# Rounded weights finished by a transfer instead of a sum: a recurrent layer and an MLP on one core

## The chip, the core and the metric

The kernel runs on one NeuronCore of a Trainium2 chip. A core has a matrix engine (PE; its weight loads are shown on a row of their own, PEld), a vector engine (DVE), an engine for activation functions (ACT), a general-purpose engine (POOL) and a sequencer for transfers (SP). Transfers between HBM and the on-chip memory (SBUF), or within it, run on 16 shared DMA engines; SP, ACT and POOL issue them, each through a queue of its own. Matrix products land in PSUM, from where DVE and ACT read them. Every engine takes its instructions in order, and waits where an instruction needs a semaphore that has not come.

The metric is the time of one execution on the device in microseconds. Before the change it is 679.25 us, the median of three runs (678.58, 679.25 and 681.2).

## The reference

Attention first: for each of 4 sequences and 8 heads, over 768 steps, a complex state of 48 x 48 decays and takes in a product of key and value, and the query reads its real part. Then an MLP with an ELU, in float32 or better:

```python
mag = np.sqrt(a_re * a_re + a_im * a_im)
scale = np.minimum(mag, 0.999) / (mag + 1e-06)
...
for t in range(S):
    ar, ai = (a_re_n[:, :, t, :, None], a_im_n[:, :, t, :, None])
    new_re = ar * S_re - ai * S_im
    new_im = ar * S_im + ai * S_re
    kv = np.einsum('bhd,bhe->bhde', k[:, :, t], v[:, :, t])
    S_re, S_im = (new_re + kv, new_im)
    y[:, :, t] = np.einsum('bhd,bhde->bhe', q[:, :, t], S_re)
...
h = x @ w_in                                           # x: 3072 x 384, w_in: 384 x 2048
g = np.where(h > 0.0, h, alpha * (np.exp(np.minimum(h, 0.0)) - 1.0))
return (g @ w_out).astype(np.float32)                  # w_out: 2048 x 384
```

The two weight matrices arrive as float64. They are rounded to float32 on the chip, from the two 32-bit words of each number.

## The kernel before

The 3072 tokens are worked through in groups `u` of 256 (two sequences of 128 steps each, so 12 groups). For each group the kernel loads q, k, v and the complex decay, forms gates from logarithms, angles and sums along time (`squares` to `gated`), transposes, scores and state products on PE (`transposed`, `scores`, `states`, `values`), moves some rows of the result into place by small transfers (`seam`, issued by POOL, ACT and SP), and passes the result `x` through the first layer (`inner`, L1202), the ELU (`elu`, L1215) and the second layer (`project`, L1225). From group 2 or 3 on the layers use sums of blocks of the weights, prepared once on DVE from the rounded ones (`summed_in`, `combined`), and fewer products.

The weights are fetched and rounded in 16 blocks of 128 partitions x 768 numbers: eight of w_in ("in" 0 to 7) and eight of w_out ("out" 0 to 7). `fetch` (L641) has SP load the raw words of a block into one of two buffers `w64` (the first blocks of "in" borrow others); a fetch waits until the block two earlier has been read. `rounded` (L647) then rounds it on DVE: `_rounded` (L36) masks and shifts the high word into a float32 `wf`, truncated (L40, L43), takes its exponent (L46) and multiplies by it the low word, scaled, which gives the rest that was cut off, `wp` (L50); a fifth step, L655, adds the two and writes the sum into w_in or w_out. That sum rounds. `wf` and `wp` come from one pool of two buffers, `wt`. `rounded` is a generator: each `convert()` in the order advances it by one step, so a block takes five of them.

The order of the work is written out by hand for the first groups: the list `first` (from L1576) names each step, and each engine receives its instructions in the order in which the list's steps issue them. A `convert` puts one instruction on DVE; an `inner` puts six matrix products on PE (one piece of 256 hidden features, `f` and `f + 1`) into one of three PSUM banks `mlp`, which the `elu` of an earlier piece must have released; an `elu` puts two instructions on ACT and one (L1221) on DVE. After the first groups the steps are ordered by due times (`put`), which the change doesn't touch. A piece `inner(u, f)` needs block f // 2 of w_in, and `project(u, n, f0, f1)` needs the blocks of w_out up to (f1 - 1) // 2. `seam(1)` issues three transfers on POOL and three on ACT.

Of the kernel before, what the change touches and what calls it, by code (L numbers as in the profile page):

```python
# [16 lines left out]
C = 128  # L17
# [14 lines left out]
WF = 2  # L32
# [3 lines left out]
def _rounded(nc, w, f, p):  # L36


    lo, hi = w[:, :, 0], w[:, :, 1]
# [466 lines left out]
def kernel(  # L506
# [140 lines left out]
    def rounded(kind, m):  # L647

        w, dst = raw.pop((kind, m))
        f = sb.tile([C, WF * DM], U32, tag="wt", bufs=2, name="wf")  # L650
        p = sb.tile([C, WF * DM], U32, tag="wt", bufs=2, name="wp")
        yield from _rounded(nc, w, f, p)
        n = dst.shape[-1]
        f, p = (x.bitcast(FP32).rearrange("p (b n) -> p b n", n=n) for x in (f, p))
        nc.vector.tensor_tensor(out=dst, in0=p, in1=f, op=ALU.add)  # L655
        done.append((kind, m))
        yield True
# [912 lines left out]
    def gates_of(u, *at):  # L1570
# [8 lines left out]
        (joined, 0, 0), (squared, "ai", 1), (joined, 0, 1), (logarithms, 0, 0),  # L1579
        (logarithms, 0, 1), (fetch, "in", 1), (fetch, "in", 2), (ratios, 0, 0), (lengths, 0, 0),  # L1580
        (warm, 2), (warm, 1), (lengths, 0, 1), (sums, 1), *2 * [(convert,)],
        (table, "exp_and_others"), (ratios, 0, 1), (powers, 0, 0), (powers, 0, 1), (warm, 2),
        (sums, 0), (warm, 1), (angles, 0, 0), (angles, 0, 1), (summed, 0), (summed, 1),
        (decayed, 0, 0), (turned, 0, 0), (decayed, 0, 1), (turned, 0, 1), (waves, 0, 0),
        (waves, 0, 1), (begun, 1), (warm, 1), (scaled, 0, "q", 0), (ends, 0), (scaled, 0, "k", 0),
        (scaled, 0, "k", 1), (scaled, 0, "q", 1), (warm, 1), (gated, 0, 0), (warm, 1), (noted, 0),
        (table, "natural_log"), (warm, 2), (gated, 0, 1), (warm, 2), *3 * [(convert,)],
        (transposed, 0, "k", 0), (transposed, 0, "q", 1), (carry_on, 0), (transposed, 0, "q", 0),
        *4 * [(convert,)], (scores, 0, 0), (transposed, 0, "k", 1), (scores, 0, 1), (load_a, 1),
        (squares, 1), (joined, 1), (fetch, "in", 3), (logarithms, 1), (states, 0, 0),  # L1590
        (values, 0, 0), (powers, 1), (convert,), (states, 0, 1), (lengths, 1), (load_qk, 1),
        (convert,), (ratios, 1), (values, 0, 1), (seam, 0), (warm, 2), (warm, 2), (decays, 1),
# [156 lines left out]
```

## Time and profile before

| | us |
|---|---|
| median of three runs | 679.25 |
| the profiled execution | 677.98 |
| its span | 676.2 |
| busy: PE, PEld | 642.4, 581.7 |
| busy: DVE, ACT, POOL | 502.3, 419.1, 157.8 |
| L655, the sum, 16 times | 0.95 each, 25.8 to 127.5 us after the span's start |
| L40 and L46, 16 times each | 0.56 each |
| L43 and L50, 16 times each | 0.96 each |

The span is what the engines' records cover; the profiled execution's time is 1.8 us longer. "Busy" counts the time in which an engine has at least one instruction under way. The records are given by line of the kernel, engine, operation and tiles (output first, then inputs). Where an engine was idle before an instruction, a bracket behind it names how long and who released it; "issue" stands for a wait that the profile puts to nobody. In the page's slices each digit is the busy share in tenths of one fortieth of the span. All rounding ends at 128.5 us.

### The profile page before, as it was taken

Reading aid. Unit: us, or ns where it says so; the run is one execution under the profiler, and the core shown is the slowest. Engines: PE = TensorE matmul, PEld = TensorE weight load, DVE = VectorE, ACT = ScalarE, POOL = GpSimd, SP = SyncE. Lnnn points to the kernel's source line nnn. Section 1 sums busy time; section 2 is a strip of 40 time slices with the busy share of each in tenths; the row PEclk is TensorE's granted clock in tenths of the full one; section 3 lists DMA queues with packets and bytes.
Section 4 is the critical chain, followed back from the end, with each engine's and each line's share of the span. In section 5 each row is a group of like instructions: output and inputs, shape, how many; then the busy total and the mean of one; then the engine's idle time right before and its main releaser. Section 6 shows DMA issues by size and latency. Waiting matters only on the chain.

```text
span 676.2 us, 17220 instructions
## 1 busy us (share of the span) xinstructions
PE 642.4 (95%) x7236; PEld 581.7 (86%) x7236; DVE 502.3 (74%) x800; ACT 419.1 (62%) x684; POOL 157.8 (23%) x200
## 2 busy tenths in 40 slices
PE   8899899999997999999999999999999999999995
PEld 6777785577896998998998998998998998999994
DVE  5889999957759678778778778778678777664481
ACT  6875455865854577677677677667677667571350
POOL 2000000122123313503503503504503503402000
PEclk9799999999998999999999999999999999999998
DMA  9995755531900452352441722441642351210000
GB/s 168 175 159 99 144 173 164 82 72 20 153 3 14 93 91 67 77 116 57 102 88 40 147 58 72 104 87 43 116 86 68 75 116 31 66 33 13 18 7 24
DMA packets 151443, 56.12 MB, mean 83 GB/s; under 512 B 129684, under 2 KB 143164, under 8 KB 151356
## 3 DMA queue, kind: packets, MB, share of 16 engines
q1 hardware_dynamic: 147616, 53.58, 39.1%
q0 software_dynamic: 3520, 1.20, 1.8%
q8 instruction: 59, 0.97, 0.6%
q14 instruction: 28, 0.23, 0.1%
q10 hardware_dynamic: 220, 0.14, 0.1%
HBM read 48.91 MB, written 4.80 MB: 79 GB/s over the span
## 4 chain that ended last, share of the span: by engine, by line
PE 53%; DVE 11%; ACT 9%; issue 4%; DMA 2%; SPq 0%; DVEq 0%; ACTq 0%
PE mlp L1319 18%; PE mlp L1450 9%; PE y L1450 6%; PE w L1023 4%; PE mlp L1210 3%; PE w L1064 3%; PE y L1109 3%; DVE g L1466 2%; PE w L837 2%; PE y L1136 2%; DVE g L1475 2%; PE mlp L1235 2%; ACT L735 2%; ACT n L746 1%; DVE g L1297 1%
## 5 line engine op out<-in xcount | busy, mean ns | idle before, releaser
L1319 PE MATMUL mlp<-w_out,g 128*128 128x192 f32 x640 | 113.3, 331 | 1.8 <-DVE ee L1332 1.8
L1319 PEld LDWEIGHTS mlp<-w_out,g 128*128 128x128 f32 x640 | 105.9, 192 | 5.5 <-DVE ee L1332 2.4
L1081 POOL TENSOR_TENSOR S<-S,T 128x384 f32<-128x384 f32 x36 | 33.6, 932 | 178.3 <-DVE S L1079 178.3
L1210 PE MATMUL mlp<-x,w_in 128*128 128x256 f32 x288 | 65.1, 381 | 2.7 <-DVE g L1221 2.4
L1210 PEld LDWEIGHTS mlp<-x,w_in 128*128 128x128 f32 x288 | 53.8, 190 | 11.3 <-DVE g L1221 2.8
L1297 DVE TENSOR_TENSOR g<-g 128x512 f32<-128x512 f32 x80 | 57.7, 731 | 5.0 <-PE mlp L1319 3.8
L1466 DVE TENSOR_TENSOR g<-g,mlp 128x512 f32<-128x512 f32 x45 | 30.7, 683 | 38.2 <-PE mlp L1450 23.9
L1450 PE MATMUL mlp<-x,w_in 128*128 128x128 f32 x432 | 57.2, 275 | 0.0
L1319 PE MATMUL mlp<-w,g 128*128 128x192 f32 x320 | 54.7, 329 | 0.0
L1475 DVE SCALAR_TENSOR_TENSOR g<-ee,g 128x512 f32<-128x512 f32 x63 | 44.1, 700 | 12.2 <-ACT ee L1472 11.9
L1450 PEld LDWEIGHTS mlp<-x,w_in 128*128 128x128 f32 x432 | 52.6, 192 | 0.0
L1319 PEld LDWEIGHTS mlp<-w,g 128*128 128x128 f32 x320 | 51.8, 190 | 0.7
L1471 ACT ACTIVATE ee<-g 128x512 f32<-128x512 f32 x63 | 39.5, 627 | 19.5 <-DVE g L1466 19.3
L1463 ACT COPY g<-mlp 128x512 f32<-128x512 f32 x36 | 21.2, 588 | 43.4 <-PE mlp L1450 43.2
L1472 ACT ACTIVATE ee<-ee 128x512 f32<-128x512 f32 x72 | 45.4, 631 | 2.3
L1190 POOL DMA_DIRECT2D x<-y x62 | 30.1, 493 | 59.4 <-ACT y L1126 37.5
L973 ACT ACTIVATE cs<-n 128x768 f32<-128x768 f32 (+1 forms) x14 | 10.5, 750 | 43.1 <-DVE n L845 43.1
L1024 ACT COPY qt<-w 128x512 f32<-128x512 f32 x48 | 25.8, 589 | 16.0 <-PE w L1023 15.9
L904 ACT ACTIVATE n<-w 64x384 f32<-64x384 f32 (+1 forms) x60 | 28.1, 486 | 8.9 <-PE w L889 8.3
L1450 PE MATMUL y<-x,w_in 128*128 128x128 f32 x216 | 29.3, 278 | 4.0 <-ACT g L1463 4.0
L1450 PEld LDWEIGHTS y<-x,w_in 128*128 128x128 f32 x216 | 26.2, 192 | 4.9 <-ACT g L1463 4.8
L1219 ACT ACTIVATE ee<-mlp 128x512 f32<-128x512 f32 x24 | 14.3, 595 | 25.6 <-PE mlp L1210 16.8
(218 smaller groups left out, 1436.8 us busy)
## 6 DMA issues: line engine op xcount, KB each, us to landing
w<-in_moe_w_out_dram SPq DMA_DIRECT2D x8, 768.0 KB, 4.4
g<-in_moe_w_in_dram SPq DMA_DIRECT2D x24, 256.0 KB, 3.0
g<-in_moe_w_out_dram SPq DMA_DIRECT2D x24, 256.0 KB, 2.9
w<-in_moe_w_in_dram SPq DMA_DIRECT2D x16, 288.0 KB, 5.7
vn<-in_v_dram SPq DMA_DIRECT2D x24, 192.0 KB, 3.9
out_dram<-o SPq DMA_DIRECT2D x48, 96.0 KB, 2.2
ar<-in_a_re_dram SPq DMA_DIRECT2D x22, 192.0 KB, 3.6
ai<-in_a_im_dram SPq DMA_DIRECT2D x22, 192.0 KB, 4.3
```

The source lines that it names most:

```text
L904: nc.scalar.activation(out=flat(x[key][to, n : n + 1]), in_=t[of], func=AF.Exp, scale=sign)
L1023: nc.tensor.transpose(t[:, h], of, ident)
L1081: eng.tensor_tensor(out=new_s, in0=new_s, in1=wide, op=ALU.mult)
L1190: eng.dma_start(out=x["x"][ds(j * HP + D, G), i], in_=x["y"][ds(j * HP + i * G, G)])
L1210: nc.tensor.matmul(t[:, e], lhsT=w_in[:, i, ts(f + e, C)], rhs=x["x"][:, i], start=(i == 0), stop=(i == NI - 1),)
L1297: nc.vector.tensor_tensor(out=S_of(u, k, h), in0=a, in1=b, op=op)
L1319: nc.tensor.matmul(to, lhsT=a[:, m], rhs=b[:, m], start=(first and h == 0 and m == 0), stop=False, skip_group_check=True,)
L1450: nc.tensor.matmul(x["c" + c][:, ts(m, C)], lhsT=a[:, m], rhs=x["mix"][p], start=(p == BANKS[c][0] and m == 0), stop=False, skip_group_che ...
L1466: nc.vector.tensor_tensor(out=part(u, to), in0=part(u, a), in1=part(u, b), op=op)
L1471: nc.scalar.activation(out=e, in_=part(u, of), func=AF.Relu, scale=-1.0)
L1472: nc.scalar.activation(out=e, in_=e, func=AF.Exp, scale=-1.0)
L1475: nc.vector.scalar_tensor_tensor(out=part(u, to), in0=nat[u]["e", to], scalar=-1.0, in1=part(u, of), op0=ALU.add, op1=ALU.max,)
```

## The change

For "in" 2 to 7 and all of "out", fourteen blocks, the fifth step is no longer a sum on DVE. The truncated part is written straight into its place in w_in or w_out (`dst`, read and written there as integers), the rest into `wp`, and POOL issues a transfer from `wp` to `dst` that adds to what stands there. Such a block takes four `convert`s: the fourth puts L50 on DVE and the transfer on POOL's queue. `wf` is no longer allocated for it, so that the two buffers `wt` hold the `wp` of two blocks. In w_in a block is three runs of 256 numbers per partition, in w_out one run of 768. "in" 0 and 1 are rounded as before.

The list `first` loses the fourteen fifth steps, and one of the `convert`s at its end that had nothing left to do. Four pieces of the first layer of group 0, `inner(0, 6)`, `inner(0, 10)`, `inner(0, 12)` and `inner(0, 14)`, stand later in it, each behind some further steps of the rounding; `inner(0, 12)` now also stands behind `inner(1, 2)`. The order of all else is kept (the list's lines are broken anew).

```diff
 def _rounded(nc, w, f, p):
-    lo, hi = w[:, :, 0], w[:, :, 1]
+    lo, hi = w[..., 0], w[..., 1]
...
     def rounded(kind, m):
         w, dst = raw.pop((kind, m))
-        f = sb.tile([C, WF * DM], U32, tag="wt", bufs=2, name="wf")
         p = sb.tile([C, WF * DM], U32, tag="wt", bufs=2, name="wp")
-        yield from _rounded(nc, w, f, p)
-        n = dst.shape[-1]
-        f, p = (x.bitcast(FP32).rearrange("p (b n) -> p b n", n=n) for x in (f, p))
-        nc.vector.tensor_tensor(out=dst, in0=p, in1=f, op=ALU.add)
+        if kind == "in" and m < 2:
+            f = sb.tile([C, WF * DM], U32, tag="wt", bufs=2, name="wf")
+            yield from _rounded(nc, w, f, p)
+            n = dst.shape[-1]
+            f, p = (x.bitcast(FP32).rearrange("p (b n) -> p b n", n=n) for x in (f, p))
+            nc.vector.tensor_tensor(out=dst, in0=p, in1=f, op=ALU.add)
+        else:
+            n = dst.shape[-1]
+            p = p.rearrange("p (b n) -> p b n", n=n)
+            each = _rounded(
+                nc, w.rearrange("p (b n) two -> p b n two", n=n), dst.bitcast(U32), p
+            )
+            for _ in range(3):
+                yield next(each)
+            for _ in each:
+                pass
+            nc.gpsimd.dma_start(out=dst, in_=p.bitcast(FP32), accum_op=ALU.add)
         done.append((kind, m))
         yield True
```

The moves, in the list (`c3.4` is the fourth `convert` of "in" 3, and so on; the names are put in here for reading):

```diff
-c3.4 (scores, 1, 0) (load_v, 2) c3.5 (fetch, "in", 5) c4.1 c4.2 ... c4.3 (inner, 0, 6) (fetch, "in", 6) (elu, 0, 2) c4.4 c4.5 c5.1 c5.2
+c3.4 (scores, 1, 0) (load_v, 2) (fetch, "in", 5) c4.1 c4.2 ... c4.3 (fetch, "in", 6) (elu, 0, 2) c4.4 (inner, 0, 6) c5.1 c5.2
...
-(inner, 0, 8) (inner, 0, 10) (elu, 0, 4) c6.3 c6.4 (elu, 0, 6) (elu, 0, 8) (fetch, "out", 0) (warm, 2)
+(inner, 0, 8) (elu, 0, 4) c6.3 c6.4 (inner, 0, 10) (elu, 0, 6) (elu, 0, 8) (fetch, "out", 0) (warm, 2)
-(inner, 1, 0) c6.5 (inner, 0, 12) c7.1 (inner, 1, 2) c7.2 c7.3 c7.4 (inner, 1, 4)
+(inner, 1, 0) c7.1 (inner, 1, 2) c7.2 c7.3 (inner, 0, 12) c7.4 (inner, 1, 4)
...
-(elu, 0, 10) c7.5 (inner, 0, 14) (elu, 1, 0) three steps of "out" 0 (elu, 0, 12)
+(elu, 0, 10) (elu, 1, 0) three steps of "out" 0 (inner, 0, 14) (elu, 0, 12)
```

## Prediction

> **What bounds the kernel now.** I read the page's slices first, then the busy time of each engine by stretches, then the order in time of PE, DVE, ACT and POOL between 24 and 140 us, where all the rounding lies, and last the transfers with their times to landing. In the slices, each 16.9 us, PE's digits are 9 nearly everywhere; DVE's are 9 in slices 4 to 7, and there alone it is as full as PE:
>
> ```profile
> PE   8899899999997999999999999999999999999995
> ...
> DVE  5889999957759678778778778778678777664481
> ```
>
> ```profile
> 60.00:80.00 20.00, 16.94 (x310) 14.64 (x310) 18.87 (x28) 10.72 (x23) 1.44 (x3) 1.00 0.72 133
> 80.00:100.00 20.00, 20.00 (x94) 17.60 (x94) 19.55 (x28) 10.09 (x17) 0.00 (x0) 1.00 0.47 147
> 100.00:120.00 20.00, 18.34 (x68) 11.79 (x70) 19.52 (x27) 12.60 (x17) 0.00 (x0) 1.00 0.63 180
> ```
>
> The columns after the length are PE, PEld, DVE, ACT, POOL, the granted clock and the transfers' share. DVE is 94 to 98% busy, but PE is full too from 80 to 100 us. A faster DVE therefore pays only where PE really waits for it. The order in time on PE shows where that is; the reader looks for the brackets:
>
> ```profile
> 61.43 2.86 PE L1210 MATMUL mlp<-x,w_in 128*128 128x256 f32 x12
> ...
> 75.81 2.86 PE L1210 MATMUL mlp<-x,w_in 128*128 128x256 f32 x12 [2.40 <-DVE g L1221]
> ...
> 78.95 23.48 PE L1210 MATMUL mlp<-x,w_in 128*128 128x256 f32 x108
> ...
> 104.08 2.85 PE L1235 MATMUL mlp<-w_out,g 128*128 128x384 f32 x8 [1.66 <-DVE g L1221]
> ```
>
> From 78.95 nine pieces of the first layer run without a gap (23.48 us, 2.6 each). The wait before 104.08 is DVE's fault: ACT had its part ready at 98.56, and DVE reached L1221 at 103.35. On the weight loads the same wait is 2.06 us; smaller ones follow at 119.77 (0.55, DVE L772) and 135.12 (0.70, DVE L1003). Together 3.3 us; after that PE is dense to 200 us. The wait before 75.81 is not the rounding's: L1221 waited for ACT, which was busy issuing transfers:
>
> ```profile
> 71.25 2.48 ACTq L1190 DMA_DIRECT2D x<-y  x3
> 73.77 0.60 ACT L1219 ACTIVATE ee<-mlp 128x512 f32<-128x512 f32 x1 [2.56 <-issue]
> ```
>
> ```profile
> 71.50 1.44 POOL L1190 DMA_DIRECT2D x<-y  x3 [16.48 <-ACT y L1126]
> ```
>
> And the rounding of block "in" 3 ends just in time. L50 and the sum L655 are its last steps on DVE, and the piece of PE at 61.43 above is the one that needs it, 0.8 us after the sum's end (60.65):
>
> ```profile
> 58.03 0.95 DVE L50 SCALAR_TENSOR_TENSOR wp<-w,wp 128x768 f32<-128x768 uint32 x1
> ...
> 59.70 0.95 DVE L655 TENSOR_TENSOR w_in<-wp,wf 128x768 f32<-128x768 f32 x1
> ```
>
> **Removed.** 14 sums on DVE, rows L655 of 0.95 us: 13.3 us of DVE, of which at most the 3.3 us of PE's waits can reach the end; the rest lies beside a full PE. I count the whole 3.3, since the sums of "in" 4 to 7 and "out" 0 to 2 (seven, 6.7 us, less 8 x 0.39 for the slower steps below) all lie before 103.35, where DVE is 4.8 us late.
>
> **Slower on DVE.** For "in" 2 to 7 the words now go straight into w_in, three runs of 256 instead of one of 768. L40 writes and L46 reads that shape. Today they take 0.56 us for 768 elements; operations that take one element at a time, L43 and L50, take 0.96. So each of the 12 costs between 0 and 0.39 us more, 0 to 4.7 in all. I take the upper end: among TENSOR_SCALAR rows, L842, whose source is no plain SBUF run, takes 0.55 us for 384 elements where L849 takes 0.36. Up to L50 of block 3 that is 4 x 0.39 - 0.95 (the sum of block 2) = +0.6, of which the 0.29 us that DVE idles at 47.35 hides half: L50 ends at 59.3 instead of 58.98. For "out" nothing changes, the destination is one run.
>
> The Trainium skill has the rule for this (VectorE: DVE Perf Modes, Mode 2×_2P): a one-source operation gets two elements a cycle only if the outermost dimensions of source and destination are even, or odd and equal. Here they are 3 and 768, so the rule says the upper end, against the change; the rows above show both rates but never this shape. With 0 in its place the sum below would be 0.3 us less.
>
> **Added: the transfer's latency.** PE's piece now waits for POOL's transfer instead of DVE's sum. Each moves 128x768 words, 393 KB, and also reads its destination. No row shows an accumulating transfer. The nearest rows:
>
> ```profile
> w<-in_moe_w_in_dram SPq DMA_DIRECT2D x16, 288.0 KB, 5.7
> ...
> x<-y POOLq DMA_DIRECT2D x62, 16.0 KB, 2.8
> ```
>
> Lower bound: the smallest POOL row, 1.8 us from issue to landing for L1190 at its median there between 30 and 240 us, plus 393 KB at the 430 GB/s that the "out" fetches reach at their peak (0.9): 2.7. Upper bound: 9 us, the longest POOL row (9.2, L862, 3 KB beside full queues). The nearest by size, pieces of 1 to 2 KB and place (44 to 78 us, beside the same fetches) is the fetch of w_in, 5.7 median, 6.4 the longest landing of L644 between 20 and 130 us; I take 6.4, since a third stream, the destination's reading, comes on top. POOL's own time is small beside it (0.49 to 0.96 us per issue, included) and POOL is idle, 0.00 busy from 80 to 120.
>
> The skill's fit for POOL's transfers (DMA: Bandwidth & Descriptors, Anatomy of one DMA) is 2.0 us plus the bytes at 436 GB/s: 2.9 us, an estimate for a plain copy. With it the two stalls below would be 0.5 and 0.0, and the sum -2.8 us, 676.5. The contended fetch row contradicts so short a time in this stretch; I follow the row.
>
> Where that latency falls on PE:
> - Block 2: L50 ends at 46.18 + 2 x 0.39 = 47.0, landing 47.0 + 0.1 + 6.4 = 53.5. Its piece starts at 51.90 now; behind it PE waits for DVE's L1003 until 55.56, some 55.9 after the shift of 0.3, and the piece takes 2.75: 0.3 us over, which I leave in the range.
> - Block 3: 59.3 + 0.1 + 6.4 = 65.8 against 61.43: PE stands 4.4 us, in order, so the transposes, scores and values of group 1 behind it stand too. PE has 0.4 us of slack there (its wait at 69.23). ACT's copies, its three issues and L1219 follow, so all up to 75.81 moves by **4.0**.
> - Block 4: L50 ends at 65.9, landing 72.4; its piece at 70.55 + 4.0 is later. Nothing.
> - Block 5: POOL must first issue the three transfers of 71.50, until 72.94. Then 72.94 + 6.4 = 79.3 against 75.81, both moved by 4.0: **3.5** us.
> - Blocks 6, 7 and "out": margins from 4 us (block 6, whose piece now comes one piece later) to over 10 us. Nothing.
>
> The wait is also on DVE: wp has two buffers, so L46 of a block waits for the transfer two blocks earlier. Behind it stand L50 and L1221, for which PE's banks wait. Between L50 of "out" 0 and L46 of "out" 2 lie 8.3 us now (88.3 to 96.5), less two sums 6.4; for "out" 4 it is 5.8. With 6.5 the stalls are 0 to 0.7 us, and DVE is ahead by then. SP's fetches are released by L50 as before; from L50 to L40 two blocks on there are 6.1 to 6.9 us now, 4.2 to 5.0 after, against 4.4 to landing: that margin is gone too, and costs up to 1 us of the 3.3 if landing gets longer. On POOL the carry of L862 and the seam's issues stand behind transfers released long before them.
>
> **Moved.** A moved piece issues six matmuls and no transfer. Three of the four pieces, 6, 10 and 14, pass only steps of DVE, ACT and SP; on PE nothing changes its order, so they are worth nothing. Piece 12 passes piece 2 of group 1 on PE: it gives block 6 another 2.6 us, which it doesn't need at 6.4.
>
> **Sum.** +4.0 + 3.5 - 3.3 = +4.2 us. The profiled execution took 677.98 (span 676.2 and 1.8 around it); it becomes 682.2. The median of the runs lies 1.27 above the profiled one, so I forecast 679.25 + 4.2 = 683.4, its own range 680.5 to 687 (landing 5 to 8).
>
> **Rivals.**
> 1. The transfer lands in under 4.5 us. Each microsecond less takes 2 off the sum: at 4.5 it is +0.4, at 3.3 -2.0: 677 to 680. For it speaks the 430 GB/s of the "out" fetches and x<-y; against it the share of the transfers of 1.10 at 60 to 62 us and 1.08 at 74 to 76.
> 2. Other side: it lands in 2.7 us and the three runs cost nothing. Then block 3 is there at 59.0 + 0.1 + 2.7 = 61.8, block 5 at 75.6, both stalls vanish, and the 0.4 of 69.23 and the 0.6 at 120.58 that the loads show as "issue" go with the 3.3: -4.3, 675. It decides below 3 us of landing. Against it: every fetch of this size here takes 3.7 us or more.
> 3. Accumulating is slow, 9 us: 6.6 and 6.1 us at blocks 3 and 5, and 2.9 at block 2 (56.1 + 2.75 against 55.9): +12.3, 691.5. Then DVE's L46 stands too. Nothing in the trace excludes it.
> 4. The fetches become DVE's bound in 80 to 115 us and the 3.3 shrinks to 1: 685.7; inside the forecast's range.
>
> **How the numbers follow.** Forecast with rival 4: 0.40, an eighth of it within 0.5% (3.4 us, about what a measurement can tell here). Rival 1: 0.25, within. Rival 2: 0.20, faster. Rival 3: 0.15. So faster 0.20, same 0.30, slower 0.50. The range goes from rival 2's 675 to nearly rival 3's end, 691.
>
> **What would show it.** L655's place on DVE is empty for 14 blocks; L40 and L46 of "in" take 0.95 us; POOL shows 14 issues, and their landing is the number on which all hangs. PE's piece 6 waits for w_in<-wp, then piece 10; the waits before "project" at 104 are gone. I am wrong if the landing is under 4.5 us, or if L1221 waits behind L46 or L40 between 80 and 115.

## The result and the profile after

The changed kernel takes 701.91 us (median of 4 runs, 699.51 to 704.76), beside 679.40 (678.58 to 681.2) for the kernel before on the same chip: a ratio of 1.0329, 95% interval 1.0283 to 1.0375. The forecast was 683.4 us with a range of 675 to 691: the sign was right, the time is 11 us above the range. The profiled execution took 699.51 us, its span is 697.8, against 676.2 before: 21.6 us to find. Lines of the kernel behind `rounded` are numbered 12 higher than before (L1222 for L1210, L1247 for L1235, L1076 for L1064).

First the page's slices of the changed kernel, 17.4 us each:

```profile
PE   8897699969999789999999999999999999999995
...
DVE  5896777855757858858858858858768768664481
PEclk9899899989999899999999999999999999999998
```

DVE is emptier, as meant, but so is PE: it has gaps in slices 4 and 5 (52 to 87 us) and in slice 9 (around 150 us). Next the order in time on PE; the columns are start, length, engine, line, operation, and in brackets the wait and who ended it:

```profile
57.46 4.27 PE L1222 MATMUL mlp<-x,w_in 128*128 128x256 f32 x12 [3.94 <-DMA w_in<-wp]
...
67.65 2.86 PE L1222 MATMUL mlp<-x,w_in 128*128 128x256 f32 x12
...
80.43 5.49 PE L1222 MATMUL mlp<-x,w_in 128*128 128x256 f32 x12 [4.05 <-DMA w_in<-wp]
87.82 2.83 PE L1222 MATMUL mlp<-x,w_in 128*128 128x256 f32 x12 [1.90 <-DMA w_in<-wp]
...
115.24 2.85 PE L1247 MATMUL mlp<-w_out,g 128*128 128x384 f32 x8 [0.84 <-DVE g L1233]
...
151.87 1.96 PE L1076 MATMUL w<-vn,kg 64*64 64x48 f32 x64 [5.58 <-DVE kg L1015]
153.76 4.80 PE L1247 MATMUL y<-w_out,g 128*128 128x384 f32 x8
```

The kernel before, at piece 8 and at the first state products of group 2:

```profile
70.55 2.86 PE L1210 MATMUL mlp<-x,w_in 128*128 128x256 f32 x12
...
135.12 1.15 PE L1064 MATMUL w<-vn,kg 64*64 64x48 f32 x64
```

The rows of the changed kernel are pieces 4, 6, 8 and 10 of the first layer, the first project piece, the first state products of group 2 and the project piece behind them. Three things stand here. PE waits for the transfers of blocks 2, 4 and 5. It waits 5.6 us at 151.87 for something that is not a transfer of the change at all. And the instructions behind a long wait are themselves slow: 4.27 and 5.49 us for pieces that take 2.75 and 2.86 before, 1.96 and 4.80 for steps that take 1.15 and 2.85. The stretches just there show why; the third column from the end is the granted clock, the next the transfers' share:

```profile
57.46:61.50 4.04, 4.04 (x12) 3.21 (x13) 2.80 (x4) 0.00 (x0) 0.94 (x1) 0.66 0.41 96
80.43:86.00 5.57, 5.49 (x12) 3.87 (x12) 3.98 (x6) 0.84 (x3) 1.26 (x1) 0.50 1.22 206
87.82:91.00 3.18, 3.18 (x17) 2.87 (x18) 3.08 (x5) 0.32 (x1) 0.00 (x0) 1.00 0.95 191
151.87:158.40 6.53, 6.53 (x72) 4.32 (x73) 5.17 (x6) 4.00 (x5) 2.30 (x2) 0.55 0.52 100
```

The clock is 0.50 to 0.66 behind the long waits and 1.00 behind the short one. The kernel before shows such a fall too, behind a wait of 4.31 us further on; the same step takes 1.45 us at 125.84:

```profile
215.00 2.90 PE L837 MATMUL w<-n,sum_turns 128*128 128x384 f32 x4 [4.31 <-DVE n L826]
```

The stretches of 20 us that the prediction showed, for the changed kernel, in the same columns:

```profile
60.00:80.00 20.00, 15.62 (x337) 13.36 (x335) 13.12 (x19) 9.47 (x21) 5.03 (x6) 0.93 0.81 126
80.00:100.00 20.00, 17.67 (x71) 14.69 (x72) 12.25 (x16) 5.98 (x11) 2.95 (x3) 0.85 0.85 177
100.00:120.00 20.00, 19.16 (x85) 15.81 (x84) 18.14 (x26) 10.00 (x17) 4.82 (x5) 1.00 0.86 220
```

DVE has 5.7 and 7.3 us less to do in the first two; PE doesn't profit, it does less too. The transfers' share in the second rose from 0.47 to 0.85.

The transfers' own view, median us from issue to landing, and the rows of L46 (count, then shortest, median and longest in ns):

```profile
w<-in_moe_w_out_dram SPq DMA_DIRECT2D x8, 768.0 KB, 6.7
...
w_out<-wp POOLq DMA_DIRECT2D x8, 384.0 KB, 6.8
w_in<-wp POOLq DMA_DIRECT2D x6, 384.0 KB, 8.1
```

```profile
L46 DVE TENSOR_SCALAR wp<-w_out x8: 559/560/561, 97.2 to 137.2; 128x768 uint32<-128x768 uint32 x8
L46 DVE TENSOR_SCALAR wp<-w_in x6: 944/946/953, 44.5 to 89.9; 128x768 uint32<-128x768 uint32 x6
```

On POOL's queue, block 2's transfer and block 5's, the latter behind the seam's three:

```profile
48.34 1.33 POOL L667 DMA_DIRECT2D w_in<-wp  x1 [6.37 <-DVE wp L50]
...
77.27 1.57 POOL L1202 DMA_DIRECT2D x<-y  x3 [3.80 <-ACT y L1138]
79.08 1.34 POOL L667 DMA_DIRECT2D w_in<-wp  x1 [0.24 <-DVE wp L50]
```

Block 2's is issued at 48.34, and the piece that needs it starts at 57.46. The six transfers of "in" landed after 9.1, 7.0, 8.2, 8.6, 7.3 and 8.0 us, the eight of "out" after 6.4, 6.4, 6.7, 8.1, 8.4, 7.4, 7.0 and 4.8. The fetches of "out", 4.4 us before at the median, now take 6.7. Only two of the eight have a known landing, so these medians rest on two each: 4.40 and 4.41 us before, 5.2 and 8.2 now, the 8.2 for the fetch issued at 114.62, between the "out" transfers. DVE feels that; the step that waits for a fetch is L40, and on SP's queue the loads of the next groups stand behind the fetches:

```profile
106.57 0.56 DVE L40 TENSOR_SCALAR w_out<-w 128x768 uint32<-128x768 uint32 x1 [0.82 <-DMA w<-in_moe_w_out_dram]
...
122.86 0.56 DVE L40 TENSOR_SCALAR w_out<-w 128x768 uint32<-128x768 uint32 x1 [3.30 <-DMA w<-in_moe_w_out_dram]
```

```profile
126.50 0.37 SPq L644 DMA_DIRECT2D w<-in_moe_w_out_dram  x1
...
128.99 5.62 SPq L598 DMA_DIRECT2D k<-in_k_dram  x2
134.72 3.27 SPq L598 DMA_DIRECT2D ar<-in_a_re_dram  x2
```

The row of ar in the kernel before:

```profile
120.64 0.99 SPq L598 DMA_DIRECT2D ar<-in_a_re_dram  x2
```

Before, the last fetch was issued at 113.69 and ar and ai of group 3 at 120.64 and 121.73, the moment their buffers came free. Now ar's buffer is free at 131.85 (the end of DVE's L771, its last reader) while SP still issues k, and ACT, which squares them before it computes the waves of group 2, waits 2.56 us for ar and 3.02 for ai. That is the wait of 5.58 on PE.

PE's lateness against before, by starts of the same instruction, adds it up: 1.4 us at the first piece (43.31 for 41.89; no transfer is waited for until then), 5.6 at piece 4, 9.9 at piece 8, 12.0 at piece 10 and at the nine dense pieces, 11.2 at the first project piece (the gain that the change was to bring: 0.8), 16.8 at the state products, 19.5 behind the slow piece, 19.2 at 230 us, 20.9 at 267 and 21.6 at the end. Of the last 2.1 us, 1.7 arise between 230 and 267 us. The 1.4 at the start and these 1.7 are falls of the clock. From 39 to 42 us the granted clock is 0.55 here and 1.00 in the kernel before; it is 1.00 also in the two runs of the changed kernel with a busy PE that follow below, which differ from it only further on, so the change does not bring that fall. At 256.57 a step behind a wait of 1.96 us for ACT takes 1.98 us and the next one 1.91; in the kernel before they take 1.16 and 1.04, behind a wait of 1.78.

### The profile page after: what moved, and what is told of

It reads as the page before. It is cut to its first block, busy times and chain, and to the rows that moved or that the text cites. A ratio compares the mean times of both kernels' runs of the same rounds, so it can differ in the third digit from the quotient of the medians.

```text
span 697.8 us, 17236 instructions
## 1 busy us (share of the span) xinstructions
PE 652.1 (93%) x7236; PEld 589.1 (84%) x7236; DVE 494.5 (71%) x786; ACT 419.7 (60%) x684; POOL 172.9 (25%) x214
## 4 chain that ended last, share of the span: by engine, by line
PE 57%; DVE 14%; DMA 11%; ACT 9%; issue 4%; SPq 3%; POOL 0%; DVEq 0%; ACTq 0%; POOLq 0%
PE mlp L1331 18%; PE mlp L1462 10%; PE y L1462 6%; PE mlp L1222 6%; PE w L1035 4%; PE w L1076 3%; PE y L1121 3%; DMA w<-in_moe_w_out_dram 3%; DMA w_in<-wp 3%; SPq L598 3%; DVE g L1478 2%; PE w L849 2%; PE y L1148 2%; DMA w<-in_moe_w_in_dram 2%; DVE g L1487 2%
## 5 line engine op out<-in xcount | busy, mean ns | idle before, releaser
L1222 PE MATMUL mlp<-x,w_in 128*128 128x256 f32 x288 | 69.2, 398 | 9.9 <-DMA w_in<-wp 9.9
L1222 PEld LDWEIGHTS mlp<-x,w_in 128*128 128x128 f32 x288 | 56.2, 199 | 20.1 <-DMA w_in<-wp 8.8
L1462 PEld LDWEIGHTS mlp<-x,w_in 128*128 128x128 f32 x432 | 52.6, 192 | 0.0
L1483 ACT ACTIVATE ee<-g 128x512 f32<-128x512 f32 x63 | 39.5, 627 | 19.8 <-DVE g L1478 19.5
L985 ACT ACTIVATE cs<-n 128x768 f32<-128x768 f32 (+1 forms) x14 | 10.5, 751 | 43.0 <-DVE n L857 42.9
L1076 PE MATMUL w<-vn,kg 64*64 64x48 f32 x1280 | 28.7, 225 | 6.3 <-DVE kg L1015 5.6
L1076 PEld LDWEIGHTS w<-vn,kg 64*64 64x64 f32 x1280 | 24.9, 139 | 11.0 <-DVE kg L1015 6.2
```

Source lines behind the costliest of these rows:

```text
L1076: nc.tensor.matmul(to, lhsT=of, rhs=vn[u % 2][ts(c, L), n, ts(h, D)], start=True, stop=True,)
L1222: nc.tensor.matmul(t[:, e], lhsT=w_in[:, i, ts(f + e, C)], rhs=x["x"][:, i], start=(i == 0), stop=(i == NI - 1),)
L1462: nc.tensor.matmul(x["c" + c][:, ts(m, C)], lhsT=a[:, m], rhs=x["mix"][p], start=(p == BANKS[c][0] and m == 0), stop=False, skip_group_che ...
L1483: nc.scalar.activation(out=e, in_=part(u, of), func=AF.Relu, scale=-1.0)
```

## The experiments

Two theories stood against each other at first: that the loss is made twice, separately, by the landing of the "in" transfers on an in-order PE and by the "out" transfers' load on the DMA engines; and that one cause, the late "in" pieces, makes all of it and the late loads are its echo. The runs are grouped by what they tell apart. Each ratio is against the kernel before, run on the same chip beside it, with its 95% interval. The kernel before had medians of 678.3 to 681.1 us in these comparisons, so kernels that ran at different times are compared by their ratios.

### The parts one at a time

The moves alone, all sums on DVE:

```diff
-(inner, 0, 6) (fetch, "in", 6) (elu, 0, 2) c4.4
+(fetch, "in", 6) (elu, 0, 2) c4.4 (inner, 0, 6)
-(inner, 0, 10) (elu, 0, 4) c6.3 c6.4
+(elu, 0, 4) c6.3 c6.4 (inner, 0, 10)
-(inner, 0, 12) c7.1 (inner, 1, 2) c7.2 c7.3
+c7.1 (inner, 1, 2) c7.2 c7.3 (inner, 0, 12)
-(inner, 0, 14) (elu, 1, 0) c8.1 c8.2 c8.3
+(elu, 1, 0) c8.1 c8.2 c8.3 (inner, 0, 14)
```

> The kernel before with the four first-layer pieces (6, 10, 12, 14) moved back as in the change; all 16 sums stay on DVE. Theory (the transfers make the whole loss): the moves are worth nothing, 679.4 us, within 1.5 of the kernel before, and piece 6 and piece 10 start where they start before (61.4 and 75.8 us, within 0.5). Rival (the order costs something by itself, for instance since piece 12 keeps a bank longer): above 684 us, with a wait of PE in front of pieces 10 to 14.

Measured: 682.06 us, ratio 1.0040 (1.0001 to 1.0080). Small, but not the nothing that was expected. DVE, which is the bound there, stands idle for 1.64 us, and the first project piece waits 2.53 us where it waited 1.66:

```profile
88.76 0.69 DVE L1221 SCALAR_TENSOR_TENSOR g<-ee,mlp 128x512 f32<-128x512 f32 x1 [1.64 <-ACT ee L1220]
```

```profile
106.10 2.85 PE L1235 MATMUL mlp<-w_out,g 128*128 128x384 f32 x8 [2.53 <-DVE g L1221]
```

The next two kernels have the moves and one kind of block by transfer. Against the changed kernel, the first has the list below; in the second the list `BY` holds the eight out blocks instead:

```diff
+    BY = [("in", 2), ("in", 3), ("in", 4), ("in", 5), ("in", 6), ("in", 7)]
...
-        if kind == "in" and m < 2:
+        if (kind, m) not in BY:         # the sum on DVE
```

> Only the blocks in 2 to 7 go by accumulating transfers; the eight out blocks keep their sum on DVE; the moves are in. Theory (two separate losses, one at the in blocks, one at the out blocks): PE waits 4 us before piece 4, 4 us before piece 8 and about 2 before piece 10, pieces 4 and 8 run at 4.3 and 5.5 us instead of 2.86, so PE is 10.5 to 12 us later at the nine dense pieces; nothing is added after that, load_a of group 3 is issued in time: 690 to 691.5 us. Rival 1 (the whole loss comes from the in blocks, the late loads being only their echo): 700 to 702 us. Rival 2 (the out transfers slow the in transfers too, or the reverse): landing of the in transfers falls under 6 us and the time under 685.

Measured: 694.13 us, ratio 1.0202 (1.0135 to 1.0269); above the expected 691.5, far from 700. The pieces that wait:

```profile
56.62 2.86 PE L1228 MATMUL mlp<-x,w_in 128*128 128x256 f32 x12 [3.53 <-DMA w_in<-wp]
...
67.46 4.47 PE L1228 MATMUL mlp<-x,w_in 128*128 128x256 f32 x12 [2.26 <-DMA w_in<-wp]
...
88.70 4.67 PE L1228 MATMUL mlp<-x,w_in 128*128 128x256 f32 x12 [8.04 <-DMA w_in<-wp]
```

The waits are neither where they were expected nor as long: 3.5 at piece 4, 2.3 at piece 6, none at piece 8, 8.0 at piece 10, together 13.8 where some 10 were expected; the nine dense pieces start at 93.65, 14.7 us later than in the kernel before (10.5 to 12 expected). The in transfers land in 7.8 us at the median, so they are not slow because of the out transfers. There is no late load, and no wait before the state products.

> Only the eight out blocks go by accumulating transfers; the in blocks keep their sum on DVE; the moves are in. Theory (the transfers load the DMA engines, the out fetches take 6.7 us to landing instead of 4.4, SP's queue passes its last fetch late, and ar and ai of group 3 come late): fetches land in 6 us or more, the last one is issued after 118 us instead of 113, PE waits 3 to 6 us in front of the state products of group 2 and runs slower behind that wait, less 1 to 2 us gained at the first project piece: 684 to 688 us. Rival 1 (the late loads need the 12 us that PE already lost): fetches as before, the waits before project gone, 676 to 678 us. Rival 2 (all loss is from the out blocks): above 695.

Measured: 689.40 us, ratio 1.0123 (1.0065 to 1.0182), 1.4 us above the expected range. The fetches of "out" take 6.5 us to landing at the median (4.45 and 8.48 us, the two known; 4.3 with the moves alone), and the late loads are here without any lateness from the "in" blocks:

```profile
144.60 1.96 PE L1082 MATMUL w<-vn,kg 64*64 64x48 f32 x64 [5.11 <-DVE kg L1021]
146.49 4.80 PE L1253 MATMUL y<-w_out,g 128*128 128x384 f32 x8
```

```profile
121.06 6.93 SPq L598 DMA_DIRECT2D k<-in_k_dram  x2
128.09 3.42 SPq L598 DMA_DIRECT2D ar<-in_a_re_dram  x2
```

So the loss is made twice; the rows show it, while the times alone do not separate the out blocks from the moves (their intervals overlap). Against the moves alone the "in" blocks cost a factor of 1.0161 and the "out" blocks 1.0083, some 11 and 6 us; with the moves' 2.7 us that is 1.0286, at the lower edge of the change's own interval. The echo theory is out.

### What makes the landing long

```diff
-            nc.gpsimd.dma_start(out=dst, in_=p.bitcast(FP32), accum_op=ALU.add)
+            nc.gpsimd.dma_start(out=dst, in_=p.bitcast(FP32))
```

> The changed kernel with plain transfers in place of accumulating ones: the rest is written over the upper part and their sum is left out. Same bytes moved, same issues, no reading of the destination. Theory (accumulating is what makes the transfer long: it must read its destination first): landing falls from 7.3 us at the median to 3 to 4.5, PE waits under 1 us before pieces 4, 8 and 10, fetches of out land in about 5 us, time 678 to 685 us. Rival (size and crowded DMA engines make it long, the accumulation adds little): landing 6 us or more, PE's waits before pieces 4 and 8 stay above 2 us, time above 692.

Measured: 691.97 us, ratio 1.0177 (1.0128 to 1.0227): between the two, half of the loss. This kernel leaves out the sum and serves only to price it. Plain transfers of the same bytes land in:

```profile
w_out<-wp POOLq DMA_DIRECT2D x8, 384.0 KB, 5.7
w_in<-wp POOLq DMA_DIRECT2D x6, 384.0 KB, 6.9
```

Accumulating adds 1.1 to 1.2 us at the median and about 0.5 to POOL's issue (1.28 for 0.79 us where there are 384 runs). The larger part is there without it: the copy for block 2 took 8.6 us where the accumulating one took 9.1. The last transfer, "out" 7, issued when the out fetches are over, lands in 4.8 us in both kernels and in 4.9 in the run with the out blocks alone (5.3 to 6.5 in three later runs). In the changed kernel the transfers' share is 1.11 during these 4.8 us, so the share alone does not set the landing. So on landing the rival is nearer, and on the time both missed. Beside the fetches is what most of these transfers have in common; that the fetches are what stretches them was not tried by itself.

Where the plain copies save time is another matter. The starts of the first project piece in the two profiles differ by 1.7 us, about the fall of the clock at the start; those of the step behind the state products and the slow piece differ by 8.5 (149.92 and 158.40). So nearly all of the saving lies at the late loads, not at the first layer. Beside plain copies the second known fetch landed in 5.1 us (8.2 beside accumulating transfers), and the wait for group 2's state products shrank to 1.70 us, behind which the clock held:

```profile
146.16 1.15 PE L1082 MATMUL w<-vn,kg 64*64 64x48 f32 x64 [1.70 <-DVE kg L1021]
```

### The clock behind a wait

The changed kernel, with PE kept busy in its waits (the results of these matmuls are overwritten):

```diff
         x["h", f] = t = ps.tile([C, 2, GT], FP32, tag="mlp", bufs=3, name="mlp")
+        for _ in range({(0, 4): 14, (0, 8): 14, (0, 10): 6}.get((u, f), 0)):
+            nc.tensor.matmul(t[:, 0, 0:C], lhsT=ident, rhs=ident, start=True, stop=True)
...
+        if (u, n) == (2, 0):
+            busy = gs[0].rearrange("p h d -> p (h d)")[:, 0:C]
+            for _ in range(20):
+                nc.tensor.matmul(busy, lhsT=ident, rhs=ident, start=True, stop=True)
```

> The changed kernel, with matmuls on the identity into the bank that is overwritten next, ahead of the places where PE waited: 14 before piece 4, 14 before piece 8, 6 before piece 10, 20 before the state products of group 2 (0.26 us each, so they fit into the waits of 3.9, 4.1, 1.9 and 5.6 us). The waits stay, PE is only kept busy in them. Theory (a long wait also lowers the granted clock, and the pieces behind it pay again: 1.4 + 2.6 us at pieces 4 and 8, 0.8 + 2.0 at the state products and the piece behind): those pieces run at 2.86, 2.86, 1.15 and 2.85 us, and the time falls by 5 to 7 from the changed kernel's 702, to 695 to 697. Rival (the low clock has nothing to do with the waits and comes by itself): the pieces stay slow in some places, the time stays within 2 us of 702.

Measured: 700.30 us, ratio 1.0317 (1.0287 to 1.0347). The pieces did as the theory says, 2.86 and 2.76 us for pieces 4 and 8. The time did not: PE came to piece 10 earlier, and waited there longer, past the six matmuls, and paid there:

```profile
87.26 5.09 PE L1234 MATMUL mlp<-x,w_in 128*128 128x256 f32 x12 [4.94 <-DMA w_in<-wp]
```

Block 5's transfer sets that start: issued 1.3 us earlier than in the changed kernel (77.78 for 79.08), it took 9.4 us to land instead of 8.6, and the piece started at 87.26 (87.82 there). At the state products the twenty matmuls ended 2.81 us before the wait did, and the two steps there stayed slow, 1.63 and 3.97 us for the expected 1.15 and 2.85. So the next kernel covers these waits as well.

```diff
-        for _ in range({(0, 4): 14, (0, 8): 14, (0, 10): 6}.get((u, f), 0)):
+        for _ in range({(0, 4): 14, (0, 8): 14, (0, 10): 26}.get((u, f), 0)):
...
-            for _ in range(20):
+            for _ in range(30):
```

> The changed kernel with PE kept busy through the whole of its four long waits: 14 matmuls on the identity before piece 4, 14 before piece 8, 26 before piece 10 and 30 before the state products of group 2. Theory (the clock falls after a wait, and what it costs at a place counts only if no later landing makes PE wait again): pieces 4, 8 and 10 run at 2.75 to 2.9 us, the state products at 1.15 and the piece behind them at 2.85; PE gains 2.2 us at piece 10 against the run with 6 there and 1.5 to 3 more behind the state products: 695.5 to 697.5 us. Rival (the granted clock falls anyway): piece 10 above 4 us, time within 2 of 700.

Measured: 698.26 us, ratio 1.0244 (1.0196 to 1.0292), 0.8 us above the expected range. Pieces 4, 8 and 10 and the two steps at the state products all run at full speed; stretches of that kernel, the same columns as above:

```profile
82.14:85.00 2.86, 2.86 (x17) 2.55 (x16) 2.79 (x5) 1.75 (x4) 0.88 (x1) 1.00 0.82 166
90.50:93.00 2.50, 2.50 (x14) 2.22 (x14) 2.43 (x3) 0.00 (x0) 0.00 (x0) 1.00 1.17 230
156.27:160.00 3.73, 3.73 (x73) 2.60 (x73) 2.62 (x4) 3.41 (x4) 1.23 (x2) 1.00 0.34 65
```

The clock falls because PE is idle, then: with the idle time filled it stays at 1.00 in the same places. What it cost in the changed kernel is 4 us by the medians (698.26 for 701.91) and 6 by the ratios (1.0244 for 1.0329); the two intervals just touch, so the time shows the sign and hardly the size. The four slow steps add up to 6.9 us. Not all of it comes back, since PE then waits for the next landing, and piece 6, whose wait of 2.69 us was not filled, now ran slow (4.54 us).

### The late loads

The kernel with the out blocks alone, with ar and ai of group 3 on POOL's queue:

```diff
-            nc.sync.dma_start(
+            (nc.gpsimd if u == 3 and name in ("ar", "ai") else nc.sync).dma_start(
```

> The kernel with only the out blocks by transfer (689.4 us), with ar and ai of group 3 loaded from POOL's queue instead of SP's. Theory (the late loads are SP's order: SP is still issuing k when ar and ai come free at 125 and 126 us): both are issued as soon as they are free, PE's wait before the state products of group 2 falls from 5.1 to under 2.5 us, those and the piece behind them run at full clock (1.15 and 2.85 us), and the time is 682 to 685 us. Rival (the DMA engines are full, share 0.93, so the loads land late from any queue): the wait stays above 4 us, the time above 687.

Measured: 684.75 us, ratio 1.0092 (1.0057 to 1.0128), for 1.0123 on SP's queue; the two intervals overlap, and the rows say more than the time. Both loads are issued as soon as they may (122.04 us, 0.6 behind the end of ar's last reader), and the steps run at full clock, but a wait between the two theories' bounds is left, 3.22 us where it was 5.11:

```profile
139.29 1.15 PE L1082 MATMUL w<-vn,kg 64*64 64x48 f32 x64 [3.22 <-DVE kg L1021]
```

```profile
133.99 0.96 DVE L1000 TENSOR_TENSOR k<-k,n 128x768 f32<-128x768 f32 x1 [3.27 <-DMA k<-in_k_dram]
```

Now it is k of group 2 that comes last, whose issue holds SP for 9.44 us (3.28 with the moves alone). So SP's order is part of it. Another part is that the loads of k are slow beside the "out" transfers, to issue and to land; the run does not show what slows them. The transfers' share while k was issued was 1.02 here and 1.11 with the moves alone, so it is not simply that the DMA engines are fuller.

### The landing under other work

The kernel with the in blocks alone, with two pieces later on PE:

```diff
-(inner, 0, 4) (gated, 1, 1) (transposed, 1, "q", 0) ... (states, 1, 0)
+(gated, 1, 1) (transposed, 1, "q", 0) ... (states, 1, 0) (inner, 0, 4)
...
-(inner, 0, 6) ... (values, 1, 1)
+(values, 1, 1) (inner, 0, 6)
```

> The kernel with only the in blocks by transfer (694.1 us), with piece 4 put behind group 1's first state products and piece 6 behind its last values, so that PE has other work while the transfers of blocks 2 and 3 are under way. Theory (the loss of the in blocks is their landing, 7 to 9 us, lying open on an in-order PE): no wait before pieces 4 and 6, about 2 us before piece 8 and about 3 before piece 10; the nine dense pieces start at 83 to 85 us instead of about 93 and 79 before, time 684 to 687 us. Rival 1 (the transfers hold DVE or the loads back, wherever PE waits): the dense pieces start after 89 us, time above 690. Rival 2 (all of it can be hidden): 679 to 682 us.

Measured: 687.69 us, ratio 1.0142 (1.0112 to 1.0172), 0.7 above the expected range, for 1.0202 with the old order. No wait at pieces 4 and 6, 0.69 at piece 8; the dense pieces start at 86.20 instead of about 93. What is left is piece 10:

```profile
81.55 4.37 PE L1228 MATMUL mlp<-x,w_in 128*128 128x256 f32 x12 [4.54 <-DMA w_in<-wp]
```

In the next kernel it goes behind the first two pieces of group 1, and a control has the same order with all sums on DVE:

```diff
-(inner, 0, 10) (elu, 0, 6) (elu, 0, 8) (fetch, "out", 0) (warm, 2) (inner, 1, 0) (convert,) (convert,) (inner, 1, 2)
+(elu, 0, 6) (elu, 0, 8) (fetch, "out", 0) (warm, 2) (inner, 1, 0) (convert,) (convert,) (inner, 1, 2) (inner, 0, 10)
```

> The kernel with only the in blocks by transfer and pieces 4 and 6 later (687.7 us), with piece 10 put behind the first two pieces of group 1 as well. Theory (what was left of the loss is the 4.5 us of waiting before piece 10 and its slow run, 4.4 instead of 2.86 us): no wait before piece 10, PE is 4 to 6 us earlier from there on, 681.5 to 684 us, within 2 of the kernel with the moves alone (682.1). Rival (DVE or the fetches are late by then and hold the dense pieces instead): a new wait of more than 3 us before one of the next six pieces, time above 685.

> The kernel before with the order of the run in which pieces 4, 6 and 10 stand later (686.8 us), and all 16 sums on DVE, no transfer at all. It prices that order. Theory (what is left of the loss of the in blocks there, 5 us against the moves alone, is the order's: the three pieces behind piece 10 wait for banks that the order frees later): PE waits about 2 us in front of the dense pieces here too, and the time is 684.5 to 687.5 us. Rival (the transfers still cost, through the two wp buffers and the fetches): no such wait, 680.5 to 683 us.

Measured: 686.83 us, ratio 1.0106 (1.0064 to 1.0149), with the transfers; 689.28 us, ratio 1.0155 (1.0106 to 1.0204), without, 1.8 us above the range expected for the control. No piece waits for a transfer longer than 0.75 us any more, but the time is above the theory's 684, with a new wait of 2.07 us, the rival's sign if not its size. The control has it too, at the same step; first the kernel with transfers, then the control:

```profile
88.38 20.69 PE L1228 MATMUL mlp<-x,w_in 128*128 128x256 f32 x84 [2.07 <-DVE g L1239]
```

```profile
89.76 19.00 PE L1210 MATMUL mlp<-x,w_in 128*128 128x256 f32 x84 [2.07 <-DVE g L1221]
```

So what remained of the loss there is the order's, not the transfers': in an order that covers the landing, the in transfers cost nothing that these runs can show. That order is no gain over the kernel before, since it costs more than it saves.

### The gain, and why so little of it came

Only "out" 0 to 2 by transfer, where the transfers' share is 0.43 to 0.53 (80 to 100 and 100 to 120 us, moves alone) and the sums hold the first project piece up:

```diff
-    BY = [("out", 0), ("out", 1), ("out", 2), ... ("out", 7)]
+    BY = [("out", 0), ("out", 1), ("out", 2)]
```

> Only out 0 to 2 go by accumulating transfers, where the DMA engines have room (share 0.43 to 0.53 before). Theory (the sums on DVE hold up only the first project piece, and the loss of the out blocks comes from the later fetches): PE's wait before the first project piece falls from 2.5 to about 1.1 us, no wait of DVE for a fetch, ar and ai of group 3 in time: 677.5 to 680.5 us, 0 to 2 below the kernel before. Rival (any transfer beside the fetches costs): DVE waits over 2 us for out 3 or 4, time above 683.

Measured: 684.09 us, ratio 1.0091 (1.0063 to 1.0119): above the theory's range, and not for the rival's reason either. PE waited 4.88 us for the first project piece. Both buffers of `wt` were still being read by the transfers of "out" 1 and 2 when "out" 3, summed on DVE and so in need of both, asked for them:

```profile
100.72 0.56 DVE L40 TENSOR_SCALAR wf<-w 128x768 uint32<-128x768 uint32 x1 [1.41 <-DMA w_out<-wp]
...
105.52 0.56 DVE L46 TENSOR_SCALAR wp<-wf 128x768 uint32<-128x768 uint32 x1 [2.50 <-DMA w_out<-wp]
```

The next kernel needs one buffer only: the other out blocks keep their upper part in w_out and are summed there, on DVE.

```diff
-            f = sb.tile([C, WF * DM], U32, tag="wt", bufs=2, name="wf")
+            if kind == "in":
+                f = sb.tile([C, WF * DM], U32, tag="wt", bufs=2, name="wf")
+            else:
+                f = dst.bitcast(U32).rearrange("p b n -> p (b n)")
...
+            f = f if kind == "in" else dst
```

> Only out 0 to 2 by transfer, and the other out blocks keep their upper part in w_out and are summed there by DVE, so that no second buffer of the pair is needed. Theory (the 4.9 us of waiting before the first project piece in the run with out 0 to 2 came from out 3's L40 and L46 waiting for buffers that the transfers still read): DVE waits for no w_out<-wp, PE's wait before the first project piece falls to 1 to 1.3 us, from 2.5 with the moves alone, and the time is 679 to 681.5 us, 0.5 to 3 below the run with the moves alone. Rival (the transfers slow the fetches even there): DVE waits 1 us or more for the fetch of out 3 or 4, PE's wait stays above 2 us, time 682 or more.

Measured: 678.73 us, ratio 0.9968 (0.9939 to 0.9997), 12 runs. The wait before the first project piece is 1.01 us; DVE waits for no transfer of the change, so the buffers were what held "out" 3; it waits 0.97 and 1.04 us for fetches, so something of the rival is there too.

Three more runs settle what the moves do, and what the gain is worth without them: piece 12's move alone, on the kernel before; the kernel just shown with no move (two of the four pieces are shown going back); and the sums in place without transfer or move.

```diff
-(inner, 1, 0) c6.5 (inner, 0, 12) c7.1 (inner, 1, 2) c7.2 c7.3
+(inner, 1, 0) c6.5 c7.1 (inner, 1, 2) c7.2 c7.3 (inner, 0, 12)
```

```diff
-(elu, 0, 4) c6.3 c6.4 (inner, 0, 10)
+(inner, 0, 10) (elu, 0, 4) c6.3 c6.4
...
-c7.1 (inner, 1, 2) c7.2 c7.3 (inner, 0, 12)
+(inner, 0, 12) c7.1 (inner, 1, 2) c7.2 c7.3
```

```diff
-    BY = [("out", 0), ("out", 1), ("out", 2)]
+    BY = []
```

> The kernel before with piece 12 alone moved behind the second piece of group 1; all sums on DVE. Theory (of the four moves only this one changes PE's order; ACT still takes piece 12's ELU first, so the ELU of the piece now ahead of it waits, and DVE, which is the bound there, stands 1.6 us before L1221): DVE idles 1.4 to 1.8 us before L1221 near 88 us, PE waits 2.2 to 2.7 us before the first project piece instead of 1.66, time 1.5 to 2.5 us above the kernel before. Rival (the four moves together, or chance): no such idle time, PE's wait under 2 us, time within 0.8 of the kernel before.

> Out 0 to 2 by transfer and the other out blocks summed in place, as in the run that was 0.3% below the kernel before, but with the four pieces where they stood before. Theory (the moves took back most of the gain): PE's wait before the first project piece is under 0.6 us, the time 1 to 2 us below that run, 2.5 to 4.5 below the kernel before, a ratio of 0.9935 to 0.9965. Rival (the gain is bounded elsewhere, by the fetches of out 3 and 4 that DVE waited 1.0 us for): the ratio stays at 0.9965 to 0.998.

> The kernel before with the out blocks' upper part kept in w_out and summed there by DVE; no transfer, no move. Control for the two runs with out 0 to 2 by transfer. Theory (what they gain is the three sums taken off DVE): same as the kernel before, a ratio of 0.998 to 1.002, PE's wait before the first project piece 1.5 to 1.8 us. Rival (the gain is the freed buffer): a ratio under 0.997 and a wait under 1 us.

Measured: piece 12's move 682.47 us, ratio 1.0037 (1.0015 to 1.0059); it alone has the 2.53 us at the first project piece, and DVE idles 2.43 us before L1221 at 91.01, more than expected. That move makes the cost of all four (1.0037 and 1.0040). On ACT, the ELU of piece 12 still stands ahead of that of the piece that now overtakes it on PE; so this ELU waits, and L1221 of DVE behind it.

Early transfers without moves: 681.30 us, ratio 1.0014 (0.9990 to 1.0037). In the profile the wait before the first project piece is gone, no bracket:

```profile
80.14 23.48 PE L1232 MATMUL mlp<-x,w_in 128*128 128x256 f32 x108
103.46 2.74 PE L1257 MATMUL mlp<-w_out,g 128*128 128x384 f32 x8
```

From the dense pieces to project it is 23.3 us, 25.1 before: 1.8 us gained there. The total doesn't show it, and the expected ratio was missed. In place without transfers: 678.64 us, ratio 0.9982 (0.9956 to 1.0007), the control, as expected the same. Its wait before project, 0.38 us, can't be compared: PE had lost 1.7 us just before, to a piece that ran at 4.54 us behind a wait of 2.79 (2.86 before, behind 2.40). One such fall of the clock is as large as the whole gain, and it comes in some executions of a kernel and not in others. So the kernel with early transfers whose ratio was 0.9968 isn't called faster than the kernel before: the same kernel without the moves' cost, which should be better still, came out at 1.0014.

## Why the prediction was wrong, point by point

The sum +4.0 + 3.5 - 3.3 failed first in its landing term, 6.4 us, which measured 7.0 to 9.1 on the blocks that PE waits for. It also put three things at nothing or left them out: block 4, the clock behind a wait, and the loads that stand behind the fetches on SP's queue. On PE's starts, the landings and the slow steps behind them made 10.6 us up to the dense pieces, the late loads and the slow steps behind those 8.3 (11.2 to 19.5); the gain was 0.8.

- **The landing.** The step was "The nearest by size, pieces of 1 to 2 KB and place ... I take 6.4". Measured: 9.1, 7.0, 8.2 and 8.6 us for blocks 2 to 5. The upper end, 9, was the better value. Of the excess over the fetch row, accumulating explains 1.1 to 1.2 us. The Trainium skill's fit for a plain transfer (DMA: Bandwidth & Descriptors, Anatomy of one DMA), from which the prediction estimated 2.9 us, is further off: the shortest plain copy took 4.8.
- **Block 2**, "0.3 us over, which I leave in the range": PE waited 3.94 us. In the run with the in blocks alone POOL issued at 47.47, close to the predicted 47.1, so the whole miss is the landing.
- **Block 3**, "PE stands 4.4 us": it didn't in the changed kernel, because block 2 had already made PE late; the predicted wait came one piece earlier. In the run with the in blocks alone it is 2.26.
- **Block 4**, "Nothing": 4.05 us. The step let only PE move back and kept L50 of block 4 at 65.9. But ahead of block 4's steps on DVE stands the masking of group 1's scores, which wait for PE (5.05 us before 65.32 in the changed kernel), so POOL issued at 72.22. In the run with pieces 4 and 6 later, PE isn't late, and POOL issued at 66.11, as predicted. The lateness of an in-order engine came back through the other engine, and so wasn't absorbed by the next piece.
- **Block 5**, 3.5 us, with POOL busy with the seam until 72.94: the issue came at 73.09 in the run with pieces 4 and 6 later, so that was right; the landing 8.3 us later wasn't.
- **The clock** was left out altogether, though the trace before has the row at 215.00; the prediction read PE's order only to 140 us. Rival 3, a landing of 9 us, came to 691.5 without it; with it the in blocks alone took 694.1. That they are so near is luck: rival 3 adds the 2.9 us of block 2 and the 6.6 of block 3, though the first delay is part of the second (without the 2.9 it comes to 688.6). In the whole change the slow steps cost about 4 to 6 us, by the run with PE kept busy. The Trainium skill has the rule (TensorE: Matmul & The Clock Gate, Part 1): after at least one idle window of about 3.4 us the clock is halved, and as long a busy stretch brings it back. The rows agree for the waits of 3.94 to 8.04 us, all followed by slow steps, and for the granted 0.50. They differ on shorter ones: behind a wait of 2.53 or 2.54 us the first project piece took 2.85 us in two of these runs and 4.27 to 4.54 in four, behind 3.53 us piece 4 took its 2.86, and behind 2.09 us a piece took 4.51 in the run with plain copies. The measured rows decide: below 3.9 us the fall comes in some executions here and not in others.
- **Blocks 6, 7 and "out"**, "Nothing", is right as far as it goes: PE waits for no transfer of those. What failed is the sentence on the fetches, "that margin is gone too, and costs up to 1 us of the 3.3 if landing gets longer". The fetches went from 4.4 to 6.7 us at the median, DVE waited 4.8 us for four of them, and the sentence stopped at DVE: behind the fetches on SP's queue stand the loads of groups 2 and 3, on them ACT's waves, and on these PE at 151.87, 5.6 us and then 2.8 of low clock. Rival 4 had the place and stopped there too, at 685.7.
- **"Moved"**, "they are worth nothing": piece 12's move costs 0.4%. I followed PE's order and not ACT's, whose ELUs kept theirs.
- **The 3.3 us of gain**: the cause was right. The wait of 1.66 us goes when the three early out sums leave DVE and nothing is moved, and with the moves the wait falls from 2.53 to 1.15 us when the out sums leave. In the change 0.8 us of it came, since piece 12's move gave DVE new idle time; of the two smaller waits, the one at 135.12 became the 5.58.
- **Small slips**: the 5.8 us between L50 of "out" 2 and L46 of "out" 4 belong to "out" 6 (for "out" 4 it is 7.0); rival 2 uses the 0.4 us at 69.23 twice; DVE's digits are 9 in slices 4 to 8. None of them moves the forecast.
- **Right**: L40 and L46 of "in" at 0.941 to 0.953 us (0.95 predicted), 0.56 for "out". The Trainium skill's rule (VectorE: DVE Perf Modes, Mode 2×_2P) said so for outermost dimensions of 3 and 768. Right were also the 0 to 0.7 us for L46 behind the transfer two blocks earlier: none waited in the change. Such waits came where a summed block follows (up to 2.50 us, and 1.99 in the run with pieces 4, 6 and 10 later).

## What to carry to other kernels

A transfer that replaces an engine's last step has a latency the engine did not have: find what lies between its issue and its first reader on every in-order queue, and take the longest landing seen beside the same traffic, not a typical one. When a stall is found, move what stands behind it on the *other* engines too and go round once more; here the second round (block 4) was as large as the first. And ask of each added transfer which fetches share the DMA engines with it, and what else waits on the queue that issues those.

## What was not expected of the hardware

- A transfer within SBUF of 393 KB from POOL's queue took 4.8 to 9.7 us to land when accumulating (4.8 to 9.1 in the changed kernel), 4.8 to 8.6 when plain; POOL was held 1.26 to 1.41 us by an accumulating one into runs of 1 KB, 0.76 to 0.80 by a plain one.
- Issuing took SP's queue longer beside the out transfers: the same two loads of k held SP for 3.28 us with the moves alone and for 5.62, 6.93 and 9.44 us in three kernels with the out transfers. The transfers' share in those moments was 1.11, 1.12, 1.00 and 1.02, so it does not tell them apart; what does is not shown.
- PE's clock after idle time cost about as much as a short stall itself: 1.4 to 2.6 us per piece of 2.86 us, avoided by matmuls on the identity (14 in 3.3 us) into a bank that is overwritten next: with them the clock stayed at 1.00.
